# Linear-attention and SwiGLU block, forward and backward on one core: the pipeline rewritten in a fixed order of emission, with the first product of the MLP's backward moved into the forward loop

## The chip, the core and the metric

The kernel runs on one core of a Trainium2 chip. Five engines work side by side, each through its own queue in order: TensorE (PE in the profile, its weight loads PEld), VectorE (DVE), ScalarE (ACT), GpSimd (POOL) and SyncE (SP), whose queue issues most of the DMAs. The metric is the time on the device in microseconds (us), lower is better. A difference under 0.3% can't be told from none.

## What is computed

One layer for 2048 tokens of width D = 640 (bf16): layer norm, linear attention with 32 heads of 20, a residual, layer norm, a gated MLP of width F = 1728, a residual; and with it the gradients for x and for the five weights, given grad_out.

```python
phi = lambda t: jnp.where(t > 0, t + 1, jnp.exp(t)) + 1e-6
pq, pk = phi(q), phi(k)
kv = jnp.einsum("bhsd,bhse->bhde", pk, v); z = jnp.einsum("bhsd->bhd", pk)
num = jnp.einsum("bhqd,bhde->bhqe", pq, kv)
den = jnp.einsum("bhqd,bhd->bhq", pq, z)[..., None] + 1e-6
A = (num / den).transpose(...).reshape(B, S, D) @ wo
MLP = (silu(hn @ w1) * (hn @ w3)) @ w2
h = x + A(layernorm(x)); h2 = h + MLP(layernorm(h))
outputs: h2, and the vjp of h2 with grad_out for x, wqkv, wo, w1, w3, w2
```

## The kernel before, in words

A tile is 128 tokens by 640 (16 tiles, ST = 16); a chunk of the MLP is 512 tokens; F is cut into FT = 14 pieces of 128 (the last has 64 rows). The stages run one after another, each with its own pools; within a stage the code emits its steps with a lag of one or two tiles, and a scheduler of the framework decides the final order on each engine.

1. Projections (F1, lines 338 to 445): normalise x, transpose it on TensorE, 15 products per 512 or 128 columns for q, k, v, the feature map phi, a transpose of phi(q) on TensorE (line 412), and phi(k)ᵀv summed per tile in `kvacc`.
2. Attention forward (F2, lines 453 to 523): num and den in one product (`nd`, line 457), division, transpose, product with wo, residual, second layer norm, transpose.
3. MLP forward (F3, lines 535 to 578): per piece of F the two products gate and up (lines 543, 546), three passes of ScalarE and five of VectorE, two stores of factors for the backward pass; then per tile the product with w2 (line 571).
4. Gradient of w2 (lines 589 to 615): first the hidden layer is transposed back on TensorE (line 593), then the product (line 607).
5. MLP backward (lines 648 to 721): grad_out is transposed on TensorE (line 651); per 256 tokens and piece of F the first product `ghh` = w2 · grad_out (line 684), two multiplications of VectorE with factors read back from memory, two stores; then `ghn`, the gradient at the normalised input (lines 698, 701), and the backward of the layer norm (lines 706 to 721).
6. Attention backward in three steps per tile, PS1 to PS3 (lines 755 to 828), the gradient of wo (line 846), then the gradients of v and k (lines 881, 896).
7. Gradient of wqkv with the transposes of the gradient of q, k, v (lines 918, 944), gradient of x (`gxn`, line 1009), and the gradients of w1 and w3 (line 994), whose second operand comes back from memory by transposing DMAs (line 977).

Products of 640 columns are issued as 512 and 128 columns. Nearly all loads and stores are issued from SyncE's queue.

## Time and profile before

| what | value |
|---|---|
| time, median of 3 runs | 1133.37 us (1130.75 to 1133.7) |
| span of the profiled execution | 1129.2 us; 4.2 us lie between it and the median |
| TensorE busy | 989.2 us, 7344 matmuls recorded |
| VectorE, ScalarE busy | 533.5 us, 359.2 us |
| mean granted TensorE clock | 0.965 |
| moved by DMA | 148.96 MB, mean 132 GB/s |

How to read it: busy time of TensorE is a modelled time of pipelined matmuls, so the start-to-start distance of equal matmuls says more than their duration. The granted clock is a share of full speed. In a row of groups or of the order of time, out<-in names the tiles, x the number of instructions. A wait is put down to what came last. A row of the table by stretches gives, for each engine, busy time and instructions in that stretch, then the clock, the DMA engines' share and the rate.

### The profile page before, as it was taken

The page shows a single profiled execution, that of the slowest core. Times are in us where ns is not written, and L with a number is a line of the kernel's source. Part 1 is how long each engine was busy: PE and PEld are TensorE (multiplying, and loading weights), DVE is VectorE, ACT ScalarE, POOL GpSimd, SP SyncE. Part 2 cuts the span into 40 slices and gives each one's busy share as a digit, 9 for nine tenths or more (in the row PEclk, how much of TensorE's full clock was granted, in tenths as well). Part 3 has the DMA queues.
Part 4 walks back from the last instruction along what each step waited for, and adds up shares of the span by engine and source line. Part 5 has one row for each costly group of instructions (what it writes and reads, how often), then busy time and mean ns, then how long its engine had stood idle before and what let it go on. Part 6 is the DMA issues. An engine that isn't in the chain of part 4 may idle for free. (4 is left out here: it accounts for less than half of the span.)

```text
span 1129.2 us, 18899 instructions
## 1 busy us (share of the span) xinstructions
PE 989.2 (88%) x7344; PEld 573.6 (51%) x7462; DVE 533.5 (47%) x1320; ACT 359.2 (32%) x595; POOL 10.9 (1%) x69
## 2 busy tenths in 40 slices
PE   3778687999999979979999999787889999899998
PEld 1445453444444455455555555464575545454554
DVE  7566696958668420035655555697062103640000
ACT  3533376735537122141111111441233223421111
POOL 3000000000000000000000000000000000000000
PEclk9999898999999999989999999798969999999999
DMA  8963345423233108475555542952473019128541
GB/s 285 308 217 134 109 152 186 142 89 106 97 99 107 61 1 192 115 184 141 158 146 145 156 121 64 245 129 58 127 175 88 27 53 232 55 73 200 140 119 40
DMA packets 257401, 148.96 MB, mean 132 GB/s; under 512 B 130848, under 2 KB 255392, under 8 KB 257312
## 3 DMA queue, kind: packets, MB, share of 16 engines
q1 hardware_dynamic: 257312, 147.76, 46.4%
q8 instruction: 58, 0.95, 0.4%
q14 instruction: 31, 0.25, 0.1%
HBM read 50.45 MB, written 67.58 MB: 105 GB/s over the span
## 5 line engine op out<-in xcount | busy, mean ns | idle before, releaser
L994 PE MATMUL gw<-gS_half,hn_sb 128*128 128x352 bf16 (+1 forms) x627 | 116.8, 345 | 5.3 <-ACT gw_ob L999 3.6
L698 PE MATMUL ghn_ps<-w1T_sb,gg_sc 128*128 128x128 bf16 (+3 forms) x438 | 109.8, 298 | 1.5 <-issue 1.1
L701 PE MATMUL ghn_ps<-w3T_sb,gu_sc 128*128 128x128 bf16 (+3 forms) x434 | 108.0, 296 | 0.2 <-issue 0.2
L994 PEld LDWEIGHTS <-hn_sb 128*128 128x128 bf16 x640 | 62.6, 98 | 59.2 <-issue 5.4
L684 PE MATMUL ghh_ps<-g2T,w2T_sb 128*128 128x256 bf16 (+1 forms) x560 | 80.6, 277 | 9.6 <-DVE gg_sc L689 9.1
L607 PE MATMUL gw2p<-g_sb,hh_sb 128*128 128x128 bf16 (+3 forms) x436 | 69.5, 299 | 13.2 <-DVE hh_sb L596 10.1
L543 PE MATMUL gate_ps<-hnT,w_sb 128*128 128x512 bf16 (+1 forms) x268 | 70.2, 386 | 2.5 <-ACT hnT L511 0.8
L546 PE MATMUL up_ps<-hnT,w_sb 128*128 128x512 bf16 (+1 forms) x280 | 70.7, 384 | 0.2
L944 PE MATMUL gwq<-g_qkv,xn_sb 128*128 128x512 bf16 (+1 forms) x309 | 67.8, 369 | 3.3 <-ACT gwq_ob L952 1.6
L1009 PE MATMUL gxn_ps<-wqkvT,g_qkvT 128*128 128x128 bf16 (+1 forms) x472 | 66.3, 301 | 5.0 <-ACT gs L1014 3.5
L684 PEld LDWEIGHTS <-w2T_sb 128*128 128x128 bf16 (+1 forms) x560 | 54.2, 100 | 30.5 <-issue 14.6
L571 PE MATMUL o_ps<-w_sb,hhT_sb 128*128 128x128 bf16 (+3 forms) x440 | 67.5, 299 | 0.7 <-issue 0.2
L688 DVE TENSOR_TENSOR gu_sc<-ghh_ps,gt_sc 128x256 bf16<-128x256 f32 x112 | 47.2, 422 | 41.7 <-PE ghh_ps L684 22.4
L552 ACT ACTIVATE sig_b<-gate_ps 128x512 bf16<-128x512 f32 (+1 forms) x56 | 33.4, 597 | 83.6 <-PE gate_ps L543 64.2
L698 PEld LDWEIGHTS <-gg_sc 128*128 128x128 bf16 x448 | 43.3, 97 | 32.3 <-issue 13.6
L357 PEld LDWEIGHTS <-xnT 128*128 128x128 bf16 x400 | 37.0, 99 | 39.7 <-issue 10.9
L607 PEld LDWEIGHTS <-hh_sb 128*128 128x128 bf16 (+1 forms) x448 | 33.8, 98 | 44.4 <-DVE hh_sb L596 12.3
L1009 PEld LDWEIGHTS <-g_qkvT 128*128 128x128 bf16 x480 | 37.3, 99 | 34.2 <-issue 6.6
L706 ACT ACTIVATE gs<-ghn_ps 128x640 bf16<-128x640 f32 x16 | 11.3, 704 | 136.4 <-PE ghn_ps L701 136.4
L701 PEld LDWEIGHTS <-gu_sc 128*128 128x128 bf16 x448 | 43.7, 98 | 20.2 <-issue 1.6
L357 PE MATMUL qkvB_ps<-wqkv_sb,xnT 128*128 128x512 bf16 (+1 forms) x235 | 45.7, 343 | 7.9 <-ACT vaug_t L404 7.7
L571 PEld LDWEIGHTS <-hhT_sb 128*128 128x128 bf16 x448 | 33.6, 97 | 35.7 <-issue 10.4
(149 smaller groups left out, 1414.8 us busy)
## 6 DMA issues: line engine op xcount, KB each, us to landing
gateT_d<-silu_b SPq DMA_DIRECT2D x52, 128.0 KB, 1.8
upT_d<-w_b SPq DMA_DIRECT2D x52, 128.0 KB, 1.8
gt_sc<-gateT_d SPq DMA_DIRECT2D x8, 832.0 KB, 5.6
ut_sc<-upT_d SPq DMA_DIRECT2D x8, 832.0 KB, 7.3
ggT_d<-gg_sc SPq DMA_DIRECT2D x104, 64.0 KB, 1.6
guT_d<-gu_sc SPq DMA_DIRECT2D x104, 64.0 KB, 1.7
w_sb<-in_B_w_dram SPq DMA_DIRECT2D x10, 432.0 KB, 4.9
vaug_d<-vaug_t SPq DMA_DIRECT2D x16, 192.0 KB, 2.1
```

The costliest lines, as they stand in the source:

```text
L357: T.matmul(outap, lhsT=xnT[t][:, c, :], rhs=wqkv_sb[:, c, n0:n0 + nw], start=(c == 0), stop=(c == DT - 1))
L543: T.matmul(gate_ps[:rows, :], lhsT=w1_sb[:, c, f0:f0 + rows], rhs=hnT[sc][:, c, :], start=(c == 0), stop=(c == DT - 1))
L546: T.matmul(up_ps[:rows, :], lhsT=w3_sb[:, c, f0:f0 + rows], rhs=hnT[sc][:, c, :], start=(c == 0), stop=(c == DT - 1))
L571: T.matmul(o2_ps[:, n0:n0 + nw], lhsT=hhT_sb[:rows, fc, t * P:(t + 1) * P], rhs=w2_sb[:rows, fc, n0:n0 + nw], start=(fc == 0), stop=(fc == ...
L607: T.matmul(pss[i][:rows, n0:n0 + nw], lhsT=hh_sb[:, t, fc * P:fc * P + rows], rhs=g2_sb[:, t, n0:n0 + nw], start=(t == 0), stop=(t == ST - 1))
L684: T.matmul(ghh[:rows, :], lhsT=w2T_sb[:, c, f0:f0 + rows], rhs=g2T[sc][:, c, :], start=(c == 0), stop=(c == DT - 1))
L688: V.tensor_tensor(out=gu_sc[:rows, fc, :], in0=ghh[:rows], in1=silub[:rows], op=ALU.mult)
L698: T.matmul(ghn[:, n0:n0 + nw], lhsT=gg_sc[:rows, fc, tt * P:(tt + 1) * P], rhs=w1T_sb[:rows, fc, n0:n0 + nw], start=(fc == 0), stop=False)
L701: T.matmul(ghn[:, n0:n0 + nw], lhsT=gu_sc[:rows, fc, tt * P:(tt + 1) * P], rhs=w3T_sb[:rows, fc, n0:n0 + nw], start=False, stop=(fc == FT ...
L944: T.matmul(pss[i][:, 0:nw], lhsT=xn_sb[:, t, m * P:(m + 1) * P], rhs=g_qkv[:, t, n0:n0 + nw], start=(t == 0), stop=(t == ST - 1))
L994: T.matmul(pss[i][:, 0:nw], lhsT=hn_sb2[:, t, m * P:(m + 1) * P], rhs=gS[:, t, n0:n0 + nw], start=(t == 0), stop=(t == ST - 1))
L1009: T.matmul(gxn[:, n0:n0 + nw], lhsT=g_qkvT[:, j, t * P:(t + 1) * P], rhs=wqkvT[:, j, n0:n0 + nw], start=(j == 0), stop=(j == QT - 1))
```

## The change

The kernel is written anew with the same products. Its order on every engine is the order in which the code emits it (`manual_schedule`).

- Projections: k, q and v are computed in products of 320 columns into three double-bank buffers; the transposes of phi(q) (line 412 before) become transposing DMAs from memory; phi(k)ᵀv is summed in PSUM over four tiles. The load of wqkv is cut into its q, k and v columns, and only two tiles of x are loaded ahead of it. The factors mq, mk and xn are no longer stored; min(phi, 1) is used in their place, and xn is computed again from x.
- Attention forward of chunk 0 is emitted between the 14 products `ghh` of chunk 0 (the "filler"); that of chunk c + 1 is spread over the pieces of F of chunk c. 1/sqrt of the layer norms is a power on GpSimd.
- MLP forward: `mlp()` does the products ghh, gate and up of one piece, five evictions by ScalarE (one for ghh), and seven multiplications or additions of VectorE; the gradients at gate and up are stored at once (`gg_d`), and the hidden layer too (`hh_d`). The product with w2 of chunk c is emitted eight matmuls at a time between the pieces of chunk c + 1.
- Gradient of w2: the hidden layer comes back by transposing DMAs (`load_hh`) instead of transposes on TensorE; its first load can only begin when the last piece has been stored.
- MLP backward's second product and attention backward run in one loop over tiles: `b_ghn(t)` in six parts of nine matmuls, between them the steps for tile t - 2 (`b_go`, `b_gndT`, `b_gkv`, `b_gpq`) and the transposes for tile t - 1. w1 and w3 are packed in 27 pieces instead of 28.
- Then the gradients of v and k between jobs of 16 matmuls for the gradients of w1 and w3, the gradient of x with further jobs between, and the gradient of wqkv last. Stores of outputs are issued from ScalarE's queue.

The diff, cut to its core:

```diff
-                T.transpose(trq[:, c * P:(c + 1) * P], pq_t[:, c * P:(c + 1) * P], ident[:])
-            V.tensor_copy(out=pqT[t][:], in_=trq[:].rearrange("p (c q) -> p c q", q=P))
...
-                    T.matmul(gate_ps[:rows, :], lhsT=w1_sb[:, c, f0:f0 + rows],
-                             rhs=hnT[sc][:, c, :], start=(c == 0), stop=(c == DT - 1))
-                for c in range(DT):
-                    T.matmul(up_ps[:rows, :], lhsT=w3_sb[:, c, f0:f0 + rows],
-                             rhs=hnT[sc][:, c, :], start=(c == 0), stop=(c == DT - 1))
-                sig_b = pf3t.tile([P, W], BF16, name="sig_b")
...
-                A.activation(sig_b[:rows], gate_ps[:rows], AF.Sigmoid)
-                A.activation(gp1_b[:rows], gate_ps[:rows], AF.Identity, bias=1.0)
-                A.copy(out=up_b[:rows], in_=up_ps[:rows])
-                V.tensor_tensor(out=silu_b[:rows], in0=gate_ps[:rows], in1=sig_b[:rows], op=ALU.mult)
...
-                SY.dma_start(out=gateT_d[f0:f0 + rows, s0:s0 + W], in_=silu_b[:rows])
...
-                V.tensor_tensor(out=w_b[:rows], in0=e_b[:rows], in1=up_b[:rows], op=ALU.mult)
-                SY.dma_start(out=upT_d[f0:f0 + rows, s0:s0 + W], in_=w_b[:rows])
...
-                T.transpose(hps[:, fc * P:fc * P + rows], hhT_sb[:rows, fc, t * P:(t + 1) * P],
-                            ident[:rows, :rows])
-            fa = min(F, 1024)
...
-                T.transpose(trg2[:, c * P:(c + 1) * P], g2_sb[:, t, c * P:(c + 1) * P], ident[:])
...
-                    T.matmul(ghh[:rows, :], lhsT=w2T_sb[:, c, f0:f0 + rows],
-                             rhs=g2T[sc][:, c, :], start=(c == 0), stop=(c == DT - 1))
-                silub = gt_sc[:, fc, :]
-                wb = ut_sc[:, fc, :]
-                V.tensor_tensor(out=gu_sc[:rows, fc, :], in0=ghh[:rows], in1=silub[:rows], op=ALU.mult)
-                V.tensor_tensor(out=gg_sc[:rows, fc, :], in0=ghh[:rows], in1=wb[:rows], op=ALU.mult)
-                SY.dma_start(out=ggT_d[f0:f0 + rows, s0:s0 + Wb], in_=gg_sc[:rows, fc, :])
-                SY.dma_start(out=guT_d[f0:f0 + rows, s0:s0 + Wb], in_=gu_sc[:rows, fc, :])
...
-                        T.matmul(ghn[:, n0:n0 + nw], lhsT=gg_sc[:rows, fc, tt * P:(tt + 1) * P],
-                                 rhs=w1T_sb[:rows, fc, n0:n0 + nw],
...
-        for t in range(1, ST):
-            if t + 1 < ST:
-                PS1(t + 1)
-            PS2(t)
-            PS3(t - 1)
...
+    ctx.enter_context(tc.manual_schedule())
...
+    dma(out=wqkv[:, :, 0:D], in_=wq_v[:, :, 0:D])
+    dma(out=x_sb[:, 2:4, :], in_=xS[:, 2:4, :])
+    dma(out=wqkv[:, :, D:2 * D], in_=wq_v[:, :, D:2 * D])
+    dma(out=wqkv[:, :, 2 * D:], in_=wq_v[:, :, 2 * D:])
...
+        q = p1_mm(t, 0)
+        if t + 2 < ST:
+            p1_norm(t + 2)
+        phi(q, pqc[g][:, i, :])
+        if t + 1 < ST:
+            p1_tr(t + 1)
+        k = p1_mm(t, D)
+        phi(k, pkc[g][:, i, :])
+        v = p1_mm(t, 2 * D)
+        A.copy(out=va[g % 2][:, i, 0:C].rearrange("p (j h e) -> p j h e", j=2, e=DA)[:, :, :, 0:DH],
+               in_=v[:, :, 0:HD].rearrange("p j (h e) -> p j h e", e=DH))
+        if t % 2 == 0 and t + 4 < ST:
+            ln1.run(x_sb, t + 4, t + 6)
+        if i == 0 and g > 0:
+            kv_group(g - 1, False)
+        if i == TPC - 1:
...
+    def mlp(c, fc, ghh):
+        if ghh is None:
+            ghp = mm5(w2T, fc, g2T[c])
+            ghh = ew("ghh")
+            A.copy(out=ghh[:], in_=ghp[:])
...
+        gp = mm5(w1, fc, hnT[c])
...
+        A.activation(sig[:], gp[:], AF.Sigmoid)
+        A.activation(s2[:], gp[:], AF.Sigmoid, scale=-1.0)
+        A.copy(out=gate[:], in_=gp[:])
+        upp = mm5(w3, fc, hnT[c])
+        A.copy(out=up[:], in_=upp[:])
...
+        V.tensor_tensor(out=gate[:], in0=gate[:], in1=sig[:], op=ALU.mult)
+        V.tensor_tensor(out=s2[:], in0=gate[:], in1=s2[:], op=ALU.mult)
+        V.tensor_tensor(out=sig[:], in0=s2[:], in1=sig[:], op=ALU.add)
+        V.tensor_tensor(out=hhT[c][:, fc, :], in0=gate[:], in1=up[:], op=ALU.mult)
+        dma(out=hh_d[f0:f0 + n, cs], in_=hhT[c][:n, fc, :])
+        V.tensor_tensor(out=gate[:], in0=gate[:], in1=ghh, op=ALU.mult)
+        dma(out=gg_d[F + f0:F + f0 + n, cs], in_=gate[:n, :])
+        V.tensor_tensor(out=sig[:], in0=sig[:], in1=up[:], op=ALU.mult)
+        V.tensor_tensor(out=sig[:], in0=sig[:], in1=ghh, op=ALU.mult)
+        dma(out=gg_d[f0:f0 + n, cs], in_=sig[:n, :])
...
+    for step in (2, (f2_ndo, 0), 2, (f2_ot, 0), (f2_ndo, 1), 1, (f2_at0, 0), 1, (f2_ot, 1), (f2_ndo, 2), 1,
+                 (f2_hn, 0), (f2_at0, 1), 1, (f2_ht, 0), (f2_ot, 2), (f2_ndo, 3), 1, (f2_hn, 1), (f2_at0, 2), 1,
+                 (f2_ht, 1), (f2_ot, 3), 1, (f2_hn, 2), (f2_at0, 3), 2, (f2_ht, 2), (f2_hn, 3), 1, (f2_ht, 3)):
+        if isinstance(step, int):
+            filler(step)
+        else:
...
+    for c in range(SC):
+        hhT[c] = pa.tile([P, FT, W], BF16, name="hhT", bufs=2)
+        o2 = o2_steps(c - 1) if c > 0 else None
+        for fc in range(FT):
+            mlp(c, fc, ghh0[:, fc, :] if c == 0 else None)
+            if o2:
+                next(o2)
+            if c + 1 < SC:
+                for f, i in sorted(side.get(fc, ()), key=lambda x: x[1]):
+                    f((c + 1) * TPC + i)
...
+    dma(out=g2[:], in_=goS)
...
+    load_hh(0)
+    for _ in o2_steps(SC - 1, A.dma_start):
...
+        if fc == 3:
+            load_hh(3)
+        if fc == 5:
+            load_w13()
+        if fc == 7:
+            load_gg(0)
+            load_gg(1)
...
+                T.matmul(acc[:, j, 0:HD], lhsT=ggb[t // 2][:, k, lo:lo + P], rhs=rhs[:, j * HD:(j + 1) * HD],
+                         start=(k == 0), stop=(k == NG - 1))
+                n += 1
+                if n % 9 == 0 and n < 54:
+                    yield
+        b_ln(acc, t)
...
+        A.activation(out=gs[:].rearrange("p (j n) -> p j n", j=2), in_=acc[:, :, 0:HD], func=AF.Identity,
...
+        A.activation(out=y[:], in_=wb[:], func=AF.Identity, bias=s[:, 3:4], scale=st.rs[:, t:t + 1])
+        V.tensor_tensor(out=out, in0=y[:], in1=res, op=ALU.add)
+
+    def b_ln(acc, t):
+        ln_bwd(acc, t, hnb[t][:], ln2, g_h[:, t, :], g2[:, t, :], br)
...
+            go = h1()
+            hs = slice(j * 16, (j + 1) * 16)
...
+                T.matmul(go[:, 0:HD], lhsT=ghT[t][:, c, :], rhs=woT[:, c, j * HD:(j + 1) * HD], start=(c == 0),
+                         stop=(c == DT - 1))
+            V.tensor_tensor(out=gv[:, hs, 0:DH], in0=go[:, 0:HD].rearrange("p (h d) -> p h d", d=DH),
+                            in1=rden[:, t, hs].unsqueeze(2).to_broadcast([P, 16, DH]), op=ALU.mult)
+        V.tensor_tensor(out=prod[:], in0=gv[:, :, 0:DH], in1=o_sb[:, t, :].rearrange("p (h d) -> p h d", d=DH),
+                        op=ALU.mult)
+        V.reduce_sum(out=gd[:], in_=prod[:], axis=AX.X)
+        V.tensor_scalar(out=gv[:, :, DH], in0=gd[:], scalar1=-1.0, scalar2=None, op0=ALU.mult)
...
+    for t in range(ST + 2):
+        g = b_ghn(t) if t < ST else wog
+
+        def part():
+            next(g, None)
+        u = t - 2
+        if t + 2 < ST:
+            b_load(t + 2)
+        if t % 2 == 0 and 2 <= t <= ST - 2 and t // 2 + 1 < ST // 2:
+            load_gg(t // 2 + 1)
+        part()
+        if u >= 0:
+            b_go(u)
+        part()
+        part()
+        if u >= 0:
+            b_gndT(u)
+        part()
+        if u >= 0:
+            b_gkv(u)
+            b_gpq(u)
+        part()
+        if 0 <= t - 1 < ST:
+            b_gT(t - 1)
+        part()
...
+        for t in range(ST):
+            T.matmul(acc[:, 0:n], lhsT=lhs[:, t, m * P:(m + 1) * P], rhs=rhs(t), start=(t == 0),
+                     stop=(t == ST - 1))
...
+    def w13_jobs():
+        for i, (_, out, f0) in enumerate(blocks):
+            load_block(i + 2)
+            for m in range(DT):
+                grad_job(hnN, m, lambda t: gb[i][:, t, :], NB, out[:, m, f0:f0 + NB])
+                yield
...
+        next(jobs)
+        gphi(vaT[c][:, :, i * P:(i + 1) * P], gkvT, pkb[t], g_k[:, t, :], d_acc)
+        next(jobs)
...
+                if j * 15 + k in (7, 15, 23) and t + 1 < ST:
+                    e_T(t + 1, (j * 15 + k) // 8)
+        gx = ex.tile([P, D], BF16, name="gx", bufs=2)
+        ln_bwd(acc, t, xnN[:, t, :], ln1, gx[:], g_h[:, t, :], ex)
+        A.dma_start(out=out1S[:, t, :], in_=gx[:])
...
+    for t in range(ST):
+        if t % 4 != 3:
+            next(jobs, None)
+        e_gxn(t)
...
+    for m in range(DT):
+        for k in range(3):
+            for j in range(2):
+                grad_job(xnN, m, half(gqkv[k], j), HD, out2S[:, m, k * D + j * HD:k * D + (j + 1) * HD])
```

Names in the rows below: `g_nd` / `gnd` is the gradient at num and den of one tile, `go_ps` / `h` the PSUM of the product with woᵀ, `prod` and `gd` lead to the gradient of den, `s`, `wb`, `y` and `gs` belong to the backward of the layer norm, which ends in `g_h`.

On VectorE, in a steady step of attention backward, the kernel before has (rows of PS2 of one tile and of PS3 of the tile ahead of it, in turn):

```order
L779 TENSOR_TENSOR g_nd<-go_ps,rden 128x32x20
L806 TENSOR_TENSOR gkvacc<-gkvacc,gkvt_ps 128x462
L782 TENSOR_TENSOR prod<-g_nd,o_sb 128x640
L806 TENSOR_TENSOR gkvacc<-gkvacc,gkvt_ps 128x294
L785 TENSOR_REDUCE gd<-prod 128x32
L816 TENSOR_TENSOR g_qkv<-gpq_ps,mq_tb 128x500
L786 TENSOR_SCALAR g_nd<-gd 128x32
L816 TENSOR_TENSOR g_qkv<-gpq_ps,mq_tb 128x140
```

and the changed kernel has in one step of its joint loop:

```order
L598 TENSOR_SCALAR s<-s 128x1
L599 TENSOR_SCALAR s<-s,ln_rs 128x1
L601 SCALAR_TENSOR_TENSOR wb<-hnb,s,gs 128x640
L604 TENSOR_TENSOR g_h<-y,g_4593 128x640
L631 TENSOR_TENSOR gnd_5311<-h_5496,rden 128x16x20
L631 TENSOR_TENSOR gnd_5311<-h_5503,rden 128x16x20
L633 TENSOR_TENSOR prod<-gnd_5311,o_sb 128x640
L635 TENSOR_REDUCE gd<-prod 128x32
L636 TENSOR_SCALAR gnd_5311<-gd 128x32
L660 SCALAR_TENSOR_TENSOR g_q<-pqb,h_5554 128x360
L660 SCALAR_TENSOR_TENSOR g_q<-pqb,h_5555 128x280
```

The layer norm's backward of tile t - 1 (the first four rows), which was in another stage, now stands on VectorE ahead of the multiplications of tile t - 2; `gkvacc` has gone.

On VectorE in the MLP's forward loop, one piece of F has before:

```order
L555 TENSOR_TENSOR silu_b<-gate_ps,sig_b 128x512
L556 TENSOR_TENSOR hhT_sb<-silu_b,up_b 128x512
L560 TENSOR_TENSOR e_b<-gp_b,silu_b 128x512
L561 TENSOR_TENSOR e_b<-e_b,sig_b 128x512
L563 TENSOR_TENSOR w_b<-e_b,up_b 128x512
```

and after, with a step of attention forward behind it (`hn` of one tile, then den and `o_t` of the next):

```order
L387 TENSOR_TENSOR gate<-gate,sig 128x512
L388 TENSOR_TENSOR s_2749<-gate,s_2749 128x512
L389 TENSOR_TENSOR sig<-s_2749,sig 128x512
L390 TENSOR_TENSOR hhT<-gate,up 128x512
L392 TENSOR_TENSOR gate<-gate,ghh 128x512
L394 TENSOR_TENSOR sig<-sig,up 128x512
L395 TENSOR_TENSOR sig<-sig,ghh 128x512
L145 TENSOR_SCALAR hn<-x_sb,ln_mv,ln_rs 128x640
L323 TENSOR_SCALAR den<-nd 128x19
L323 TENSOR_SCALAR den<-nd 128x13
L324 RECIPROCAL rden<-den 128x32
L326 TENSOR_TENSOR o_t<-nd,rden 128x380
```

The two multiplications of the backward pass (rows L392 and L395) and the side chain of the next chunk are now in the forward loop.

On SyncE's queue at the end of the MLP's forward loop, before, the transposed w2 is what follows the last outputs:

```order
L575 DMA h_t_4626<-h_d 128x640
L578 DMA out_dram<-h_t 128x640 x3
L619 DMA_TRANSPOSE w2T_sb<-in_B_w_dram 128x5x1728
L615 DMA out_dram<-gw_ob 128x640 x3
L635 DMA_TRANSPOSE w1T_sb<-in_B_w_dram 128x13x640
```

and after, the last stores of the hidden layer and of the gradients, then grad_out and the hidden layer's transposed loads, then the weights for the next loop:

```order
L391 DMA hh_d<-hhT 64x512
L393 DMA gg_d<-gate 64x512
L396 DMA gg_d<-sig 64x512
L414 DMA out_dram<-h_4446 128x640
L472 DMA g_4593<-in_grad_out_dram 128x16x640
L478 DMA_TRANSPOSE hb<-hh_d 128x16x512 x3
L478 DMA_TRANSPOSE hb<-hh_d 128x16x192
L495 DMA w13tail<-in_B_w_dram 128x5x64
L496 DMA w13tail<-in_B_w_dram 128x5x64
L497 DMA_TRANSPOSE w13a<-in_B_w_dram 128x13x640
```

What the gradient of w2 needs is now behind the last store of the loop on this queue, where the kernel before had its operand in SBUF.

1479 lines of the change are left out of this document (576 added, 903 removed).

## Prediction

> **What bounds the kernel now.** I read the page's totals first, then busy time by stretches cut at the stages, then single rows for prices.
>
> ```profile
> span 1129.2 us, 18899 instructions
> PE 989.2 (88%) x7344; PEld 573.6 (51%) x7462; DVE 533.5 (47%) x1320; ACT 359.2 (32%) x595; POOL 10.9 (1%) x69
> ...
> GB/s 285 308 217 134 109 152 186 142 89 106 97 99 107 61 1 192 115 184 141 158 146 145 156 121 64 245 129 58 127 175 88 27 53 232 55 73 200 140 119 40
> ```
>
> TensorE is the busiest, yet it can't be all of it. A product's true price is the distance between starts:
>
> ```profile
> 241.28 1.25 PE L543 MATMUL gate_ps<-hnT,w_sb 128*128 128x512 bf16 x5
> ...
> 243.45 1.24 PE L543 MATMUL gate_ps<-hnT,w_sb 128*128 128x512 bf16 x5
> ...
> 991.61 8.10 PE gxn_ps L1009 x59
> ```
>
> Ten products of 512 columns (five of L543, five of L546 between) take 2.17 us: 217 ns each, 0.424 ns a column. The gxn row agrees: 59 products, half of 512 and half of 128 columns, 137 ns on average for 320. From the shapes in the code the kernel before streams 2,107,520 columns, 894 us; so some 235 us of the span are waits, half clock and narrow products. The stretches tell where:
>
> ```profile
> core 0: us, PE busy (x) PEld busy (x) DVE busy (x) ACT busy (x) POOL busy (x), PEclk, DMA share, GB/s
> 0.00:20.00 20.00, 1.40 (x11) 1.19 (x12) 13.48 (x48) 6.22 (x7) 10.93 (x69) 1.00 0.83 270
> 20.00:128.00 108.00, 84.53 (x621) 51.03 (x628) 67.08 (x171) 45.20 (x63) 0.00 (x0) 1.00 0.64 218
> 128.00:191.00 63.00, 46.79 (x536) 31.27 (x545) 53.99 (x181) 40.09 (x65) 0.00 (x0) 0.94 0.39 133
> 191.00:388.00 197.00, 194.05 (x988) 88.99 (x1007) 135.24 (x296) 94.14 (x170) 0.00 (x0) 0.99 0.33 110
> 388.00:429.00 41.00, 30.12 (x309) 20.58 (x314) 11.54 (x17) 11.19 (x15) 0.00 (x0) 1.00 0.01 5
> ...
> 491.00:705.00 214.00, 199.36 (x1500) 125.26 (x1522) 118.04 (x315) 36.14 (x61) 0.00 (x0) 0.99 0.53 143
> 705.00:789.00 84.00, 64.09 (x703) 44.12 (x712) 66.57 (x142) 28.81 (x56) 0.00 (x0) 0.87 0.57 141
> ...
> 833.00:849.00 16.00, 14.82 (x251) 12.75 (x247) 13.86 (x33) 1.12 (x2) 0.00 (x0) 0.50 0.33 104
> ```
>
> The start (20 us with 1.4 us of products), attention forward (VectorE busy 54 of 63 us: 3.4 us a tile) and attention backward (67 of 84) are not TensorE's; between dense stages it waits and then runs at half clock (0.50 in the last row). The mean clock of 0.965 costs at most 0.035 x 1129 = 40 us.
>
> **The change, part by part.** *Removed columns.* The transposes of phi(q) (10,240), of the hidden layer (27,648) and of grad_out (10,240), one of 28 pieces of ghn (10,240) and 5,248 of small ones: 63,616 columns, 27 us. 2,043,904 remain, 867 us: the floor. On it I set, stage by stage, what TensorE still waits for. Prices of VectorE and ScalarE:
>
> ```profile
> L556 DVE TENSOR_TENSOR hhT_sb<-silu_b,up_b 128x512 bf16<-128x512 bf16 x52 | 22.1, 425 | 5.0 <-DVE silu_b L555 0.5
> L278 DVE BATCH_NORM_STATS2 bnst<-x_sb 128x6 f32<-128x320 bf16 x32 | 13.5, 463 | 4.9 <-DMA x_sb<-in_A_x_dram 4.9
> L380 DVE SCALAR_TENSOR_TENSOR pq_t<-qkvA_ps,mq_t 128x640 bf16<-128x640 f32 x16 | 13.1, 820 | 0.1
> L376 DVE TENSOR_SCALAR mq_t<-mq_t 128x640 bf16<-128x640 bf16 x16 | 5.1, 318 | 1.9 <-ACT mq_t L375 1.8
> L779 DVE TENSOR_TENSOR g_nd<-go_ps,rden 128x640 bf16<-128x640 f32 x16 | 13.1, 819 | 6.2 <-PE go_ps L772 6.2
> L782 DVE TENSOR_TENSOR prod<-g_nd,o_sb 128x640 bf16<-128x640 bf16 x16 | 8.0, 502 | 0.1
> L785 DVE TENSOR_REDUCE gd<-prod 128x32 f32<-128x640 bf16 x16 | 13.0, 814 | 0.1
> L786 DVE TENSOR_SCALAR g_nd<-gd 128x32 bf16<-128x32 f32 x16 | 3.7, 230 | 0.0
> ...
> L552 ACT ACTIVATE sig_b<-gate_ps 128x512 bf16<-128x512 f32 x52 | 31.1, 597 | 80.8 <-PE gate_ps L543 63.6 <-DVE e_b L561 14.3 <-PE up_ps L546 1.0
> L706 ACT ACTIVATE gs<-ghn_ps 128x640 bf16<-128x640 f32 x16 | 11.3, 704 | 136.4 <-PE ghn_ps L701 136.4
> ```
>
> *Start and projections.* Two tiles of x (0.33 MB) and the q columns (0.82 MB) now lead; v, last of the weights, has 3.1 MB up to its end, 11 us at 285 GB/s, about 13 with issue. Tile 0 is done at 15.5 us. A further tile is 30 products of 320 (0.136 us each), five transposes (54 ns each) and a quarter of a kv group: 4.7 us; VectorE has 2 x 0.46 + 0.2 statistics, 0.32 normalising, 2 x (0.32 + 0.82) phi and 0.27 sums, 4.0. With three double banks the bunched statistics show a little: 5.0, for 15 tiles 75. Before it was 128 us up to here, now 90.5. The stores of xn, mq and mk that go lay beside this work (DMA share 0.64 in row 20), so they gain nothing.
>
> *Attention forward of chunk 0 with the filler.* Products 14 x 1.085 + 4 x 2.22 = 24.1 us, last kv group 1.3, waits 3: 28. The power on GpSimd has no row. Its nearest ones there are 0.2 us (10.9 us in 69 instructions); at 2 us each the chain hn to its transpose would wait some 4 us in this chunk, and later chunks give it a whole piece of F. I take 0.6, in the 3.
>
> *MLP forward.* Seven passes of VectorE at 0.425 are 2.97 us a piece, the next chunk's side chain 4 x 3.4 / 14 = 0.97: 3.94. Products in chunk 0 (gate, up, side) only need 2.8, so VectorE sets 14 x 3.94 = 55, with waits 57. In chunks 1 and 2 products are 15 x 0.217 + 8 x 0.136 + 0.64 = 4.98 a piece against 4.2 (VectorE) and 3.4 (ScalarE, five evictions at 0.59 and two of the side chain): 70, with a little at the side steps 71 each. Chunk 3 lacks the side: 60.8. The last products with w2: 112 x 0.136 = 15.2.
>
> *Gradient of w2.* The transposes (41 us with their waits, row 388) go; its operand now comes by DMA behind the last store.
>
> ```profile
> w2T_sb<-in_B_w_dram SPq DMA_TRANSPOSE x1, 11.4
> ```
>
> That is 2.21 MB at 194 GB/s, so the first 2.10 MB of the hidden layer take 10.8 us; grad_out ahead of it 2.62 MB, 9; VectorE's last piece ends 3.9 us after its products. 23.7 less the 15.2 us that cover it: 8 us of wait; none if both loads run side by side, 12 if stores hold them up. The Trainium skill (DMA: Bandwidth & Descriptors, "Latency and other measured facts") gives a DMA transpose 261 GB/s; by that the wait is 5.5 and the total 2.7 us lower; the row above has less. The products: 448 x 0.136 = 60.9. The weights and first gradients for the next loop (some 9.5 MB from the fourth piece on) are about as long as the 43 us left, so that ScalarE's eviction of kvbdT, behind an output that waits in the same queue, is late: 7 (3 to 12).
>
> *The joint loop.* Products of a step: ghn 54 x 0.136 = 7.34, go 1.36, transposes 0.60, kv and gpq 0.63: 9.93 us. But VectorE is in order. The layer norm's backward of tile t - 1 before:
>
> ```profile
> 602.24 0.70 ACT L706 ACTIVATE gs<-ghn_ps 128x640 bf16<-128x640 f32 x1 [3.65 <-PE ghn_ps L701]
> ...
> 605.39 0.92 ACT L719 ACTIVATE ybuf<-wbuf,s,rstd 128x640 bf16<-128x640 f32 x1 [2.36 <-DVE wbuf L716]
> ...
> 606.34 0.49 DVE L721 TENSOR_TENSOR g_h_sb<-ybuf,g_sb 128x640 bf16<-128x640 bf16 x1
> ```
>
> From gs to its end 4.6 us, 0.3 of them another row: 4.3 and 0.1 from the last product. Behind it, and behind VectorE's wait for ScalarE's y, are queued the two multiplications by rden, prod, gd and the last small row, 2.2 us; TensorE's transposes of gnd wait for these and can start 6.6 us after ghn(t - 1). TensorE arrives there after 9 + 18 parts of ghn and go: 27 x 0.136 + 1.36 = 5.0. So each step waits 1.6: 11.5 x 14 = 161. Two first tiles 15, two last steps with gwo's parts 21, the rest of gwo 8.7: 206.
>
> *Then* a wait for the transposed loads of pk, v and the first gradient block, which start late behind buffers of the loop: 4 (0 to 12). Gradients of v and k with jobs of 16 x 0.122 = 1.95: 5 jobs and transposes 10.8, 16 x (0.63 + 3.9) = 72.5, 1.5 of waits. Three jobs and the wait for wqkvT 7.7. gxn with its transposes 16 x 4.89 = 78.2, 12 jobs 23.4, and 6 where ScalarE, waiting to issue the store of gx, evicts a transpose late. Eight jobs 15.6, wqkv 480 x 0.136 = 65.3, end 3.5. Six hand-overs of PSUM between stages, 0.7 each (row L706): 4.
>
> The sum: 15.5 + 75 + 28 + 57 + 142 + 60.8 + 15.2 + 8 + 60.9 + 7 + 206 + 4 + 84.8 + 7.7 + 107.6 + 15.6 + 65.3 + 3.5 + 4 = 968 against a span of 1129.2. The median stands 4.2 above its profile: **972 us**.
>
> **The rivals.** *Unbroken products:* the chains hide better than VectorE's rows say (they overlap by some tens of ns); the joint loop's wait (22), half of chunk 0's excess over its products (9) and half the loads' waits (10) go: 931. For it, VectorE has 17 us spare in a loop step's order; against it, the order puts y's wait ahead. *Exposed loads:* at the four hand-overs with transposed loads (hidden layer, weights, pk and v, wqkvT) I count 20 us together; if no load runs beside another they triple: 1012; the row 705 at 141 GB/s and a DMA share of 0.57 show that the queue is not free there. *Half clock, slower:* the joint loop idles in each step, and if this drops the clock as in the row 833 (0.50 at 14.8 of 16 us busy), its 184 us of products double: 1156. It decides if the loop's clock stays under about 0.53; above that the change is still faster. Against it, the row 20 to 128 idles 23 us in short waits at clock 1.00. The Trainium skill (TensorE: Matmul & The Clock Gate, "A second HAM failure mode: psum-queue depth-cycling") holds that micro-idles between groups of products do make the clock swing; that same row disagrees. *Not as it says:* none of the transposes is put back and the order is written out, so I give this nothing.
>
> **How the numbers follow.** My forecast (955 to 995) 0.45, unbroken products (920 to 955) 0.2, exposed loads (995 to 1040) 0.25, half clock in the whole loop 0.03, the rest, mostly between 1040 and 1130, 0.07. The range 930 to 1040 leaves about 0.15 out. 0.3% (3.4 us) is what a measurement tells from none; faster 0.96, same 0.01, slower 0.03.
>
> **What would show it.** First products near 8 us and F1's end near 91; VectorE over 90% busy in chunk 0, TensorE in chunks 1 to 3; in the joint loop a wait of transposes of gnd for VectorE of 1 to 2 us in each of 14 steps; 5 to 10 us before the gradient of w2. Wrong it is if products of 320 columns come slower than 140 ns apart, if chunk 0 takes over 75 us, or if the loop's clock is far from 1.

## The result and the profile after

The changed kernel takes **1004.5 us** (median of 4 runs, 1001.4 to 1007.4) against 1132.8 us before (1130.8 to 1133.7): ratio 0.887, 95% interval 0.884 to 0.890. The profiled execution took 1007.4 us with a span of 1005.6 us. The forecast was 972 us, so the direction and the order of size came as said, and 32 us are missing. The time lies outside the 955 to 995 us that the prediction called its own forecast, and inside the band (995 to 1040) that it gave to exposed loads.

First the totals and two rows of the page's 40 slices, TensorE's busy tenths and its granted clock, of the changed kernel:

```profile
span 1005.6 us, 16837 instructions
PE 902.2 (90%) x6741; PEld 614.0 (61%) x6741; DVE 458.2 (46%) x1162; ACT 383.0 (38%) x682; POOL 24.5 (2%) x43
...
PE   5999888899999999699888888889899898888998
...
PEclk9999988999999999799999999999899999999999
```

603 recorded products fewer, no slice of the middle below 0.6 of PE, and no clock below 0.7 in any slice. By stretches, the gain of 124 us in the span is: projections 128 to 89.5 us; attention forward and MLP forward, up to the last product with w2, 260 to 314.8 (they now hold the MLP backward's first product, 280 x 0.217 = 60.8 us of TensorE); all that follows 741 to 601.3. The removed columns are 27 us of the gain by the prediction's count; the other 97, by subtraction, are waits, half clock and narrow products, and no run splits them.

Busy time of the stretches that the prediction priced (columns: from and to, length, then PE, PEld, DVE, ACT, POOL busy, granted clock, DMA share, GB/s):

```profile
8.60:89.40 80.80, 78.01 (x636) 57.66 (x636) 61.84 (x140) 42.37 (x63) 13.43 (x19) 1.00 0.84 238
89.40:119.90 30.50, 25.23 (x178) 14.31 (x176) 18.50 (x56) 13.28 (x23) 2.21 (x4) 1.00 0.30 102
119.90:182.00 62.10, 48.47 (x248) 23.45 (x248) 51.97 (x143) 35.62 (x65) 2.58 (x4) 0.88 0.53 161
...
481.00:697.00 216.00, 187.65 (x1553) 136.64 (x1552) 93.52 (x216) 54.30 (x85) 0.00 (x0) 0.98 0.44 112
...
805.60:937.00 131.40, 119.26 (x1010) 90.16 (x1011) 44.27 (x112) 63.42 (x111) 0.00 (x0) 0.99 0.26 68
```

The rows are the projections, attention forward of chunk 0, chunk 0 of the MLP, the joint loop, and the gxn stage with its jobs. What TensorE waited for, from the list of its waits (total, times, longest):

```profile
PE h1b L641 <- DVE gnd L636: 27.2, 15, 1.9
PE trq L836 <- ACT gT L837: 10.3, 14, 1.6
PE tr L334 <- ACT hnT L360: 9.0, 11, 1.0
PE tr L359 <- DVE hn L145: 8.4, 4, 3.1
PE gw L519 <- DMA hb<-hh_d: 8.0, 1, 8.0
...
PE gxn L843 <- DMA wqT<-in_A_wqkv_dram: 5.5, 1, 5.5
PE job L756 <- DMA gb<-gg_d: 5.0, 1, 5.0
```

Four of these seven lines are TensorE standing in its written order behind an operand that another engine is late with; three are loads.

### The profile page after: what moved, and what is told of

It reads as the page before. It is cut to its first block, busy times and chain, and to the rows that moved or that the text cites. A ratio compares the mean times of both kernels' runs of the same rounds, so it can differ in the third digit from the quotient of the medians.

```text
span 1005.6 us, 16837 instructions
## 1 busy us (share of the span) xinstructions
PE 902.2 (90%) x6741; PEld 614.0 (61%) x6741; DVE 458.2 (46%) x1162; ACT 383.0 (38%) x682; POOL 24.5 (2%) x43
## 4 chain that ended last, share of the span: by engine, by line
PE 62%; DVE 15%; ACT 8%; DMA 8%; SPq 3%; issue 2%; ACTq 1%; POOL 0%; DVEq 0%
PE mm L365 16%; PE job L756 16%; PE ghn L582 7%; PE o L407 5%; PE big L216 4%; PE gxn L843 3%; ACT y L603 2%; DVE wb L596 2%; DMA hb<-hh_d 2%; PE gw L519 2%; DVE wb L601 2%; ACT gs L593 2%; PE at L342 2%; PE gwo L670 2%; DMA ggb<-gg_d 2%
## 5 line engine op out<-in xcount | busy, mean ns | idle before, releaser
L365 PE MATMUL mm<-hnT,w 128*128 128x512 bf16 x560 | 135.5, 391 | 0.9 <-ACT hnT L360 0.9
L756 PE MATMUL job<-gb,hnN 128*128 128x288 bf16 x960 | 127.9, 288 | 7.1 <-DMA gb<-gg_d 5.0
L756 PEld LDWEIGHTS <-hnN 128*128 128x128 bf16 x960 | 92.5, 98 | 30.9 <-DMA gb<-gg_d 5.2
L582 PEld LDWEIGHTS <-ggb 128*128 128x128 bf16 x864 | 82.9, 98 | 31.0 <-issue 0.5
L843 PE MATMUL gxn<-wqT,gT 128*128 128x320 bf16 x480 | 76.1, 303 | 5.5 <-DMA wqT<-in_A_wqkv_dram 5.5
L216 PE MATMUL big<-wqkv,xnT 128*128 128x320 bf16 x480 | 71.4, 306 | 4.5 <-DVE pqc L224 2.8
L365 PE MATMUL mm<-g2T,w2T 128*128 128x512 bf16 x280 | 69.9, 382 | 0.0
L582 PE MATMUL ghn<-w13a,ggb 128*128 128x320 bf16 x448 | 69.7, 304 | 0.0
L407 PE MATMUL o<-w,hhT 128*128 128x320 bf16 x448 | 67.9, 299 | 1.0 <-DVE h L412 1.0
L582 PE MATMUL ghn<-w13b,ggb 128*128 128x320 bf16 x416 | 63.8, 299 | 0.0
L387 DVE TENSOR_TENSOR gate<-gate,sig 128x512 bf16<-128x512 bf16 x56 | 23.7, 423 | 53.8 <-ACT gate L382 53.6
```

The lines of the kernel that those rows point to most:

```text
L216: T.matmul(acc[:, j, 0:HD], lhsT=xnT[t][:, c, :], rhs=wqkv[:, c, n0 + j * HD:n0 + (j + 1) * HD], start=(c == 0), stop=(c == DT - 1))
L365: T.matmul(acc[:], lhsT=w[:, c, fc * P:(fc + 1) * P], rhs=rhs[:, c, :], start=(c == 0), stop=(c == DT - 1))
L387: V.tensor_tensor(out=gate[:], in0=gate[:], in1=sig[:], op=ALU.mult)
L407: T.matmul(o2["ps"][:, 0:HD], lhsT=hhT[c][:, fc, i * P:(i + 1) * P], rhs=w2[:, fc, j * HD:(j + 1) * HD], start=(fc == 0), stop=(fc == FT - 1))
L582: T.matmul(acc[:, j, 0:HD], lhsT=ggb[t // 2][:, k, lo:lo + P], rhs=rhs[:, j * HD:(j + 1) * HD], start=(k == 0), stop=(k == NG - 1))
L756: T.matmul(acc[:, 0:n], lhsT=lhs[:, t, m * P:(m + 1) * P], rhs=rhs(t), start=(t == 0), stop=(t == ST - 1))
```

## The experiments

All times below stand against the changed kernel's 1004.5 us; each ratio is against the kernel before, on the same chip. The theory they began with: the gain is fewer columns plus waits that the fixed, spread-out order hides. The first rival: the removed work does it, and the order hardly matters.

**The order left to the scheduler**

```diff
-    ctx.enter_context(tc.manual_schedule())
```

> Edit: the one line that keeps the written order is taken out, so the framework's scheduler sets the order of the same instructions. Theory (the gain is 27 us of removed columns and the rest is waits hidden by where the side chains, old products and jobs stand between dense products): 40 us or more is lost against the changed kernel's 1004.5, so 1045 to 1110, ratio to the kernel before 0.92 to 0.98. Rival (the gain is the removed work, the earlier start and the loads; any order that keeps the dependences does): within 15 us of 1004.5, ratio 0.875 to 0.90.

Measured: **943.9 us**, ratio 0.834 (0.833 to 0.835). Both expectations fall, the theory's by its sign: the same instructions in the framework's order are 60 us faster than in the written one. The time comes out of the stages with in-order waits, where an engine stands at one instruction while later ones that don't need it are queued behind. Its list of waits and three stretches (chunk 0; joint loop with gwo; gxn stage):

```profile
PE h1b L640 <- DVE gnd L635: 9.7, 14, 1.0
...
PE gw L518 <- DMA hb<-hh_d: 5.0, 1, 5.0
...
PE tr L358 <- DVE hn L144: 1.4, 2, 0.9
PE trq L835 <- ACT gT L836: 1.3, 2, 1.1
```

```profile
123.10:169.00 45.90, 45.27 (x270) 23.33 (x269) 43.40 (x136) 34.88 (x65) 2.63 (x4) 1.00 0.46 144
451.00:647.00 196.00, 185.14 (x1559) 135.63 (x1559) 92.76 (x218) 55.52 (x88) 0.00 (x0) 1.00 0.44 115
752.80:871.10 118.30, 117.03 (x1009) 90.13 (x1010) 44.71 (x112) 63.21 (x111) 0.00 (x0) 0.98 0.28 75
```

Chunk 0 takes 48 us from its first product to chunk 1's (62.7 in the written order), chunk 1 66 (73.5), the joint loop 196 (216), the gxn stage 118 (131): 55 of the 66 us between the two profiled executions. It is not better everywhere: TensorE waits 11.6 us for the first normalised x (6.1 in the written order), and chunk 0 begins 3.2 us later. In the joint loop the scheduler put the last addition of the layer norm's backward (line 603 here) two rows later on VectorE, behind the two multiplications that do not need it, and there it waits 0.27 us:

```profile
502.15 0.89 DVE L630 TENSOR_TENSOR gnd<-h,rden 128x320 bf16<-128x320 f32 x2
503.31 0.49 DVE L603 TENSOR_TENSOR g_h<-y,g 128x640 bf16<-128x640 bf16 x1 [0.27 <-ACT y L602]
503.72 0.50 DVE L632 TENSOR_TENSOR prod<-gnd,o_sb 128x640 bf16<-128x640 bf16 x1
```

**The side chain in one block, in the written order and in the scheduler's**

```diff
-        for k, fs in ((3 * i, (f2_nd, f2_o)), (3 * i + 1, (f2_ot,)), (3 * i + 2, (f2_at,)),
-                      (3 * i + 3, (f2_hn,)), (3 * i + 4, (f2_ht,))):
-            side.setdefault(k, []).extend((f, i) for f in fs)
+        for fs in ((f2_nd, f2_o), (f2_ot,), (f2_at,), (f2_hn,), (f2_ht,)):
+            side.setdefault(FT - 1, []).extend((f, i) for f in fs)
```

> Edit: the attention forward of the next chunk (side chain) stands in one block behind the last piece of each of chunks 0 to 2, and not spread over its pieces. Theory: the block is bound by VectorE's chain, as attention forward in the kernel before (63 us for four chunks' tiles of 16, 3.4 us of VectorE a tile): three blocks of four tiles, each tile 1 to 4 us of wait on TensorE, some half clock behind them, and in chunk 0 some of VectorE's load moves out of the pieces: 20 to 50 us slower than 1004.5. Rival: under 5 us.

Measured in the written order: **1094.4 us**, ratio 0.967 (0.964 to 0.969), 90 us slower, so 70% of the gain of 128 us is gone; more than the 20 to 50 expected. Chunk 0, then the first block:

```profile
121.80:163.00 41.20, 33.63 (x142) 14.40 (x142) 31.89 (x82) 27.94 (x54) 0.00 (x0) 0.92 0.65 192
163.00:211.00 48.00, 21.94 (x111) 11.59 (x109) 22.81 (x65) 7.55 (x12) 2.19 (x4) 0.53 0.15 48
```

The block takes 48 us, with no engine busy for as much as half of them, at a clock of 0.53, while the pieces without the side chain take 41.2 us and not 62.7. In the block TensorE waits 26.0 us for four tiles, 6.5 a tile where the expectation had 1 to 4; these waits and the half clock are what it had too small.

With the scheduler's order, by the same line as in the first experiment:

> Edit: the side chain in one block, as in the run of that name (1094.4 us), but the line that keeps the written order is out, so the scheduler sets the order. Theory, formed after the scheduler's order came out at 943.9 (what is written decides only because the scheduler is off; with it, the same work runs at the same time from either text): within 10 us of 943.9, ratio 0.825 to 0.845. Rival (the scheduler follows the written order too, as a priority, so spreading it still pays): 30 us or more above 943.9, ratio over 0.86.

Measured: **954.1 us**, ratio 0.842 (0.840 to 0.843). The two texts that are 90 us apart in their written order are 10 apart under the scheduler: at the theory's edge. Nine tenths of what spreading by hand gains here, it gains only because the scheduler is off.

**The products with w2, and the fused product, in blocks**

```diff
-        o2 = o2_steps(c - 1) if c > 0 else None
+        o2 = None
+        for _ in o2_steps(c - 1) if c > 0 else ():
+            pass
```

> Edit: the 112 products with w2 of the chunk before stand as one block ahead of chunks 1, 2 and 3, and not eight at each piece. Theory: a block of 15.2 us is dense in itself and covers the end of the elementwise chain of the chunk before, but then a piece of chunks 1 and 2 has 15 x 0.217 + 0.64 = 3.9 us of products against VectorE's 3.94 and 3.4 of ScalarE, so that VectorE sets the pace as in chunk 0: 3 to 15 us slower than 1004.5. Rival (spreading does nothing): within 3 us.

Measured: 1013.9 us, ratio 0.896 (0.894 to 0.897): 9 us slower, inside the theory's 3 to 15. TensorE's waits for hn are 13.2 us in 12 places against 8.4 in 4; whether VectorE sets the pace there, as the theory says, was not read further. Blocks of five pieces for the fused product:

```diff
-            mlp(c, fc, ghh0[:, fc, :] if c == 0 else None)
+            if c > 0 and fc % 5 == 0:
+                blk5 = []
+                for f in range(fc, min(FT, fc + 5)):
+                    acc = mm5(w2T, f, g2T[c])
+                    blk5.append(pa.tile([P, W], BF16, name="ghh", bufs=6))
+                    A.copy(out=blk5[-1][:], in_=acc[:])
+            mlp(c, fc, ghh0[:, fc, :] if c == 0 else blk5[fc % 5][:])
```

> Edit: the fused product (gradient at the hidden layer, five products of 512 columns a piece) is kept in the forward loop but stands in blocks of five pieces ahead of them for chunks 1 to 3, with six buffers. Theory: the fusion itself is kept, but a block is 5.4 us of products without elementwise work beside it, and the four other pieces then have 10 x 0.217 + 8 x 0.136 + 0.64 = 3.9 us of products against VectorE's 3.94: 5 to 25 us slower than 1004.5. Rival: the buffers make up for it, under 4 us.

Measured: 1005.1 us, ratio 0.888 (0.885 to 0.890), no change: the rival holds. Whether it matters that the product is in the loop, this run does not tell; in blocks of five or one by one made no difference.

**What bounds the chunks: less on VectorE, more on TensorE**

The first kernel leaves out a factor of chunk 0's gradient and the second counts a product twice, so both serve for their times alone.

```diff
-        V.tensor_tensor(out=sig[:], in0=sig[:], in1=ghh, op=ALU.mult)
+        if c > 0:
+            V.tensor_tensor(out=sig[:], in0=sig[:], in1=ghh, op=ALU.mult)
```

> Edit: chunk 0 leaves out one of VectorE's seven passes (sigmoid term times the gradient at the hidden layer), so the gradient at the gate of chunk 0 lacks that factor; the rest is as in the changed kernel. Theory of the prediction (VectorE's 3.94 us a piece set chunk 0): 14 x 0.425 = 6 us less, chunk 0 from 62.1 to 56, the whole 5 to 7 us faster than 1004.5. Rival (the in-order waits of TensorE for the side chain's hn, hnT and o_t set it, since VectorE is busy only 52 of 62 us): under 2 us.

Measured: 995.7 us, ratio 0.879 (0.876 to 0.881), 9 faster. Chunk 0 goes from 62.7 to 56.7 us: the 6 that were expected, so VectorE's passes are on the path in chunk 0. The other 3 us, beyond the expected 5 to 7 in all, lie outside chunk 0, and the runs of one kernel here spread by that much and more.

```diff
-        gp = mm5(w1, fc, hnT[c])
+        gp = ps.tile([P, W], F32, name="mm", bufs=3)
+        for n, d in enumerate((0, 0, 1, 2, 3, 4)):
+            T.matmul(gp[:], lhsT=w1[:, d, fc * P:(fc + 1) * P], rhs=hnT[c][:, d, :], start=(n == 0), stop=(n == 5))
```

> Edit: each piece of the MLP forward has one product of 512 columns more (the gate counts its first fifth twice), 56 in all, 12.2 us of TensorE by the changed kernel's 0.217 us each. Theory (TensorE's columns are the price in chunks 1 to 3, VectorE and waits in chunk 0): 42 x 0.217 = 9.1 us slower than 1004.5, 3.0 in each of chunks 1 to 3, under 1 in chunk 0. Rival 1 (TensorE has slack everywhere): under 3 us. Rival 2 (TensorE's own chain sets chunk 0 too): 12 us, 3 of them in chunk 0.

Measured: 1011.4 us, ratio 0.893 (0.891 to 0.896), 7 slower. From chunk 0's start to the last product with w2 it is 8.9 us longer (293.5 against 284.6), 0.4 of it in chunk 0 and 8.5 in chunks 1 to 3, against the theory's 9.1: a column costs nearly what the prediction took where TensorE is the bound.

**The late addition in the joint loop**

```diff
-        V.tensor_tensor(out=out, in0=y[:], in1=res, op=ALU.add)
+        def add():
+            V.tensor_tensor(out=out, in0=y[:], in1=res, op=ALU.add)
+        return add
...
+        if t - 1 in late:
+            late.pop(t - 1)()
```

> Edit: in the joint loop alone, the last addition of the layer norm's backward (it waits for ScalarE's y) stands behind the five rows of go on VectorE and not ahead of them. Theory (TensorE's 27 us of waits there, 1.8 in each of 15 steps, are VectorE's in-order wait for y): the wait for gnd falls below 0.5 us a step, the loop from 216 to 190 to 200, the whole 15 to 26 us faster than 1004.5. Rival (the chain of go, prod, gd and gnd itself is as late, or the loop is held by its loads): under 5 us, the wait stays over 1.2 us a step.

Measured: **981.3 us**, ratio 0.866 (0.864 to 0.869), 23 us faster. One step of the changed kernel, from the timeline (start, length, engine, line; in brackets the wait ahead):

```profile
560.83 0.92 ACT L603 ACTIVATE y<-wb,s,ln_rs 128x640 bf16<-128x640 f32 x1 [2.10 <-DVE wb L601]
...
561.78 0.49 DVE L604 TENSOR_TENSOR g_h<-y,g 128x640 bf16<-128x640 bf16 x1 [1.07 <-ACT y L603]
562.19 0.88 DVE L631 TENSOR_TENSOR gnd<-h,rden 128x320 bf16<-128x320 f32 x2
563.11 0.51 DVE L633 TENSOR_TENSOR prod<-gnd,o_sb 128x640 bf16<-128x640 bf16 x1
563.65 0.82 DVE L635 TENSOR_REDUCE gd<-prod 128x32 f32<-128x640 bf16 x1
564.50 0.24 DVE L636 TENSOR_SCALAR gnd<-gd 128x32 bf16<-128x32 f32 x1
564.80 0.51 PE L641 MATMUL h1b<-ident,gnd 128*128 128x128 bf16 x6 [1.87 <-DVE gnd L636]
```

VectorE stands 1.07 us at the addition for y, with five rows behind it that TensorE waits for. With the addition behind them the step goes from 12.0 to 10.5 us:

```profile
PE h1b L645 <- DVE gnd L640: 4.3, 14, 0.3
```

**Three waits for loads and stores**

Grad_out's rows loaded at the third piece of chunk 3:

```diff
+            if fc == 2 and c == SC - 1:
+                g2 = U1.tile([P, ST, D], BF16, name="g2", tag="Q")
+                dma(out=g2[:], in_=goS)
...
-    g2 = U1.tile([P, ST, D], BF16, name="g2", tag="Q")
-    dma(out=g2[:], in_=goS)
```

> Edit: the load of grad_out's rows (2.62 MB) is issued at the third piece of chunk 3 and not ahead of the transposed load of the hidden layer. Theory (the 8.0 us wait ahead of the gradient of w2 comes from the two loads in a row behind the last store): the wait falls to 0 to 3 us, the whole 5 to 9 us faster than 1004.5. Rival (the wait is the transposed load's own 11 us and the last stores of the hidden layer): the wait stays at 6 to 9, the whole within 3 us.

Measured: **993.1 us**, ratio 0.878 (0.875 to 0.880), 11 faster, more than the 5 to 9 expected. The products of the gradient of w2 start as those with w2 end (405.4 us; no wait), take 61.5 us and not 63.7, since the clock no longer drops behind a wait, and the next loop's wait shrinks from 4.8 to 2.4.

The store of gx by SyncE:

```diff
-        A.dma_start(out=out1S[:, t, :], in_=gx[:])
+        dma(out=out1S[:, t, :], in_=gx[:])
```

> Edit: the stores of gx in the last loop but one are issued by SyncE and not by ScalarE. Theory (10.3 us of TensorE's waits there, for the eviction of transposes into gT, come from ScalarE standing at the store, which waits for VectorE's last addition): these waits fall below 3 us, the whole 6 to 11 us faster than 1004.5. Rival (ScalarE is late by its own order of evictions, or the clock is what costs): waits stay over 7 us, the whole within 3 us.

Measured: 1001.6 us, ratio 0.883 (0.881 to 0.886), within the uncertainty of no change. The expected waits go and most of the gain is eaten: the 14 waits became 5, but one of them is new.

```profile
PE trq L836 <- ACT gT L837: 8.9, 5, 5.9
```

```profile
850.34 0.34 SPq L849 DMA_DIRECT2D out_dram<-gx  x1
...
850.78 5.26 SPq L736 DMA_TRANSPOSE gb<-gg_d  x1
...
856.14 0.53 SPq L831 DMA_DIRECT2D x_t<-in_A_x_dram  x1
...
858.75 0.45 DVE L145 TENSOR_SCALAR xnN<-x_t,ln_mv,ln_rs 128x640 bf16<-128x640 bf16 x1 [8.44 <-DMA x_t<-in_A_x_dram]
...
862.63 0.69 PE L836 MATMUL trq<-ident,g_v 128*128 128x128 bf16 x5 [5.91 <-ACT gT L837]
```

Behind the store a transposed load holds SyncE's queue for 5.26 us, the next tile of x comes behind it, VectorE's normalising waits for x, and ScalarE and TensorE wait for VectorE. In the changed kernel, with no store of gx ahead of it on this queue, the same load goes out at 843.84 us and holds the queue for 4.42, and no wait for gT there is over 1.6 us.

Three jobs moved to the wait for the transposed wqkv:

```diff
         e_T(0, k)
         next(jobs, None)
+        next(jobs, None)
```

> Edit: three of the products for the gradients of w1 and w3 (jobs, 1.95 us each) move from behind the loop of gxn to the three transposes ahead of it. Theory (5.5 us of wait for the transposed wqkv, and half clock for 6.8 us behind it, are uncovered time): the wait goes, 4 to 9 us faster than 1004.5. Rival (the wait only moves, to the load of the first gradients or to the end of that stage): within 2 us.

Measured: 999.2 us, ratio 0.881 (0.878 to 0.885), between both, and unclear: the interval overlaps that of the changed kernel. In the profile TensorE's wait for the transposed wqkv is gone and the jobs behind the loop take 11.8 us and not 17.7, but the loop itself takes 116.3 and not 113.8, and its waits for gT are 13.0 us and not 10.3: 3.4 us are left.

**All of them, with the scheduler's order outside the joint loop**

The edit is the four above together, and:

```diff
-    ctx.enter_context(tc.manual_schedule())
...
+    fixed = tc.manual_schedule()
+    fixed.__enter__()
     for t in range(ST + 2):
...
+    fixed.__exit__(None, None, None)
```

> Edit: the scheduler sets the order everywhere but in the joint loop, which keeps the written order with the last addition late; with it the early load of grad_out's rows, the stores of gx issued by SyncE, and three jobs moved to the wait for the transposed wqkv. Theory (these waits are apart from each other, and the scheduler had not removed them): from the scheduler's 943.9, 6 us less in the joint loop (its products took 161.7 us with the late addition against 167.8), 5 at the hidden layer's load, 5 at wqkv's, 1 to 3 elsewhere: 922 to 932, ratio 0.814 to 0.824. Rival (each wait moves to the next load): 938 or more.

Measured: **942.4 us**, ratio 0.831 (0.830 to 0.833), the lowest median of all, but only 1.6 us below the scheduler alone by the medians and 3 by the ratios: the rival holds.

```profile
PE trq L845 <- ACT gT L846: 8.1, 3, 4.7
PE gw L519 <- DMA hb<-hh_d: 5.0, 1, 5.0
...
PE gwo L674 <- DVE g_h L605: 2.3, 1, 2.3
```

Each gain is given back nearby. The products of the joint loop take 162.4 us and not the 167.8 of the scheduler alone, but gwo behind them 31.1 and not 27.6, partly waiting for the last late addition. The wait of 5.4 us for wqkv is gone and the jobs behind the gxn loop take 9.8 and not 15.7, but that loop 112.1 and not 102.8: its waits for gT are 8.1 us, as in the run with the stores on SyncE, where the scheduler alone had left 1.3. So the expectation that the scheduler had not removed these waits was wrong for gT. The wait for the hidden layer is 5.0 as under the scheduler alone; why the early load does not shorten it there stays open.

## Why the prediction came out as it did, point by point

*Floor and columns:* right. The run with one product more in each piece gives 8.5 us for 9.1 in chunks 1 to 3, and the last stage, 480 products with nothing beside them, took 65.2 us against 65.3.

*Start and projections:* right, the projections' first products at 8.6 and their end at 89.5 us (90.5 said).

*Attention forward of chunk 0:* 30.4, 2.4 over. The power on GpSimd, which I had between 0.2 and 2 us and took as 0.6, has its row now:

```profile
136.53 0.68 POOL L142 TENSOR_TENSOR ln_rs<-ln_ve,mhalf 128x1 f32<-128x1 f32 x1 [19.04 <-DVE ln_ve L140]
```

*"VectorE sets 14 x 3.94 = 55, with waits 57":* the step that failed in kind. Chunk 0 took 62.7, and VectorE was busy 51.97 of 62.10 us, 84% and not over 90. VectorE's passes are on the path (the run without one shows it), and the rest is a ring of waits through three in-order engines, VectorE, TensorE and ScalarE:

```profile
138.88 0.43 DVE L395 TENSOR_TENSOR sig<-sig,hhT 128x512 bf16<-128x512 bf16 x1
139.22 0.44 DVE L145 TENSOR_SCALAR hn<-x_sb,ln_mv,ln_rs 128x640 bf16<-128x640 bf16 x1
...
139.72 0.45 PE L359 MATMUL tr<-ident,hn 128*128 128x128 bf16 x5 [1.97 <-DVE hn L145]
...
145.46 0.42 DVE L387 TENSOR_TENSOR gate<-gate,sig 128x512 bf16<-128x512 bf16 x1 [1.49 <-ACT gate L382]
```

The normalising of hn stands behind all seven passes of a piece, TensorE stands 1.97 us at the transpose for it, so the next piece's products are late, and VectorE then waits 1.49 us for ScalarE's eviction of them. I had priced VectorE as a sum of 55 and the waits as 2 us in all; it was busy 52 and stood some 10. The clock is in it too, which I left at full speed for this chunk: 248 recorded products take 48.47 us at 0.88 here, where 270 take 45.27 at 1.00 under the scheduler. Under the scheduler, with the passes taken apart, chunk 0 takes 48. The ring is read from these rows; no run moves the normalising alone.

*Chunks 1 to 3:* 204.5 against 202.8, right; TensorE was 97% busy in chunk 1. *Products with w2:* 17.4 (15.2). *Wait for the hidden layer:* 8.0, the number said, and for the reason said: the early load of grad_out removes it. The exact number is luck: the operand was there 25.6 us after chunk 3's last product and not 23.7, and the products with w2 that cover it took 17.4 and not 15.2, so two errors cancel. *Gradient of w2:* 63.7 (60.9), the difference being half clock behind that wait, 2.2 us of which go with it. *Next loads:* 4.8 (7).

*The joint loop, "each step waits 1.6: 11.5 x 14":* the mechanism was right to the row and its size nearly: 1.8 us in each step, with products of 10.2 (9.93 said), so 12.0 us a step. With a start of 16.6 (15) and 31.0 at the end (29.7) the loop took 216 and not 206. The prediction had blamed the order (VectorE stands at y's addition) and taken it as given; one moved row is worth 23 us.

*The wait behind the joint loop and the gradients of v and k:* 93.7 (88.8); the wait for the first gradient block alone is 5.0. *"Three jobs and the wait for wqkvT 7.7":* 14.7. The load's issue, and the row ahead of it on SyncE's queue:

```profile
786.43 4.75 SPq L736 DMA_TRANSPOSE gb<-gg_d  x1
791.27 11.61 SPq L823 DMA_TRANSPOSE wqT<-in_A_wqkv_dram  x1
```

It landed at 805.6 us, when the products begin. The last product that reads what its slot held before starts at 786.5 us, but the load goes out 4.8 us later, directly behind a transposed load of a gradient block that holds the queue for 4.75; three jobs cover a part of the rest. A load of 2.46 MB, and what stands ahead of it on its queue, needed a price of their own in the sum. *The gxn stage with its jobs:* 131.5 (123.2). ScalarE's standing at the store was the right cause (waits of 10.3 us against the 6 said, most of them gone with the store on another queue).

*PSUM hand-overs, 4 us:* none seen apart. The misses add up: -1 + 2.4 + 5.7 + 1.7 + 2.2 + 2.8 - 2.2 + 10.2 + 4.9 + 7 + 8.3 - 4 - 0.4 = 37.6, the 1005.6 of the span against 968. Against the forecast 32.5 us are missing and not 37.6, since the 4.2 us that I had added between span and median did not come: the profiled execution was the slowest of the four, and the median stands 1.1 below its span.

*The rivals.* Half clock in the joint loop did not come (0.98). Exposed loads named a time near the measured one (1012), but not its cause: the waits at the four hand-overs, 8.0, 4.8, 5.0 and 5.5, are 23 us where I counted 20, and no tripling: that the time fell into this rival's band is chance. Unbroken products (931) is what the scheduler nearly reaches with this work, 944. The 17 us that I called spare on VectorE in a loop step can't be: a step is 12.0 us long, and VectorE is busy for 93.5 of the loop's 216. "None of the transposes is put back and the order is written out, so I give this nothing" was right as to work. What I never weighed is that a fixed order takes the scheduler away, and what that costs here: 60 us.

How much of the 124 us belongs to the fusion and how much to the earlier start, against the kernel before, no run takes apart; that was not tried.

## What to carry to other kernels

An order written by hand is a claim about every engine's queue: before keeping it, run the same program with the scheduler's order and compare the list of waits; here the work was worth 188 us under the scheduler, and the written order took 60 of them back. Look for an instruction that waits on another engine with rows behind it that do not need it: one row moved gave 23 us. Moving a store or a load to another queue needs a look at what is queued behind it there, since these edits, put together with the scheduler's order, gave next to nothing: each gain was given back nearby.
